# A GpSimd copy on 15 rows in place of two zero stores: backward pass of a decode block

## The chip, the cores and the metric

The kernel runs on one core of a Trainium2 chip. The core has five engines, TensorE (PE), VectorE (DVE), ScalarE (ACT), GpSimd (POOL) and SyncE (SP), and 16 DMA engines that move data between its on-chip memory and HBM. The metric is the time of one execution on the device in microseconds, taken as the median of the runs; smaller is better. Everything is bf16 unless said otherwise.

## The reference, cut to what matters

The forward pass is a residual block for one new token of each of 4 batches: layer norm, attention of 32 query heads over a cache of 8 kv-heads, and a gated MLP beside it. The attention looks at the last `W` = 1024 of `Sk` = 4096 cached keys alone.

```python
W = min(4096, max(256, Sk // 4))                       # 1024
k = jnp.repeat(k_cache[:, :, Sk - W:, :], rep, axis=1)
v = jnp.repeat(v_cache[:, :, Sk - W:, :], rep, axis=1)
p = _softmax(jnp.einsum("bhqd,bhkd->bhqk", q, k) * (Dh ** -0.5), axis=-1)
o = jnp.einsum("bhqk,bhkd->bhqd", p, v)
return x + A(layernorm(x)) + B(layernorm(x))
# ... (projections, gelu, transposes left out)

_out, _vjp = jax.vjp(_f, A_x, A_k_cache, A_v_cache, A_wq, A_wo, B_w_gate, B_w_up, B_w_down)
_grads = _vjp(grad_out)
return (_out0, *grads)
```

What must be written is the output and the gradient of every input. The gradients of the two caches, `out_2` (dk) and `out_3` (dv), have the caches' shape (4, 8, 4096, 128), 33.5 MB each. For the first `K0` = 3072 keys of every head the gradient is zero, because the attention never looks at them. These zero regions, 786,432 bytes for each batch and kv-head of each tensor, have to be written all the same.

## The kernel before: the parts that matter here

A zeroed tile in on-chip memory is the source of all zeros. One store writes the zero regions of two kv-heads of one batch: 128 partitions of 6144 elements (12,288 bytes) each. There are 32 such stores, listed in `zlist`, dk and dv in turn, batch by batch. They are issued by SyncE in small numbers between the other stores, to keep the DMA queue filled.

```python
ZR = 2
ZW = K0 * Dh * ZR // P                                  # 6144
ztile = const.tile([P, ZW], BF16, name="ztile")
zlist = deque((og, b, g) for b in range(B) for g in range(0, G, ZR) for og in (out_2, out_3))

def zero(n=1):
    for _ in range(min(n, len(zlist))):
        og, b, g = zlist.popleft()
        store(nc.sync, og[b, g:g + ZR, 0:K0, :].rearrange("g (m j) d -> m g (j d)", m=P // ZR), ztile[:], "zeros")

nc.gpsimd.memset(ztile[:], 0.0)
zero(3)
# ...
```

The helper `store` issues a DMA from the given engine; stores of the kind "zeros" and of the kind "rest" are declared to write disjoint parts.

```python
def store(eng, out, in_, kind):
    eng.nop()
    d = eng.dma_start(out=out, in_=in_)
    for k in ("rest", "zeros") if kind == "rest" else ("rest",):
        tc.declare_no_dep(d.ins, group=k, reason="stores write disjoint parts of the outputs")
    tc.add_to_no_dep_group(kind, d.ins)
    return d
```

The attention goes through the kv-heads in `NT` = 4 steps of two heads. A step transposes the keys and values, computes the softmax and its gradient, and leaves pieces of the large outputs in `bg`, from which `tick` takes some at later points. Pieces of dv and dk (`stg_dv`, `stg_dk`, 1 MB a store, three staging buffers) end with one zero store; those of the weight gradients are `osb_o` and `osb_q` (512 KB a store).

```python
def piece(g, j, held):                                  # of dv and dk
    # ... matmul into PSUM, evac into stg
    if j == JQ - 1:
        store(nc.sync, og[:, t * GP + g, K0:Sk, :].rearrange("b (m j) d -> m b (j d)", j=JB),
              stg[:].rearrange("p j d -> p (j d)"), "rest")
        zero()
# ...
for t in range(NT):
    kv_steps(t, 0, 0)
    # ...
    softmax(t)
    kv_steps(t, 1, 1)
    if t == NT - 1:
        zero(4)
    link(len(chain))
    softmax_d(t)
    link()
    odq(t, 0)                                           # ends with two multiplies on GpSimd (o_s)
    load_kv(t + 2, 1)                                   # nothing for the last two steps
    # ...
    fin(t)
    # ...
    (k0, k1), (o0, o1, q0, q1) = dvdk(t, 1), dw(t)
    for p in (k0, o0, k1, o1, q0, q1):
        bg.extend(p)
tick(len(bg))
zero(len(zlist))
# ... the sums for out_0 and out_1, stored from ScalarE with four rows each
```

GpSimd issues DMAs of its own in one place: the loads of the weights of steps 1 to 3 (`wo_sb`, `wq_sb`, 128 rows each).

Of the kernel before, what the change touches and what calls it, by code (L numbers as in the profile page):

```python
# [14 lines left out]
P = 128  # L15
# [3 lines left out]
def kernel(  # L19
# [28 lines left out]
    nc = tc.nc  # L48

    B, Sq, D = A_x.shape  # L50
    _, G, Sk, Dh = A_k_cache.shape
# [4 lines left out]
    K0 = Sk - W  # L56
# [4 lines left out]
    NT = G // GP  # L61
# [38 lines left out]
# [8 lines that stand above are left out]
# [12 lines left out]
    def load_w(t, eng=nc.gpsimd):  # L120
        pool = w_pool[t % 2]
        wo_t[t] = pool.tile([P, HG, D], BF16, name="wo_sb", tag="wo")
        eng.dma_start(out=wo_t[t][:], in_=wo_v[t])
        wq_t[t] = pool.tile([P, ND, CW], BF16, name="wq_sb", tag="wq")
        eng.dma_start(out=wq_t[t][:], in_=wq_v[t])

    def load_kv(t, k):
        if t >= NT:
            return
        d_, src, nm = ((k_t, A_k_cache, "kb"), (v_t, A_v_cache, "vb"))[k]  # L130
        for g in range(GP):
            tl = kv_pool[t % 2].tile([P, JB, Dh], BF16, name=nm, tag=nm)
            nc.sync.dma_start(out=tl[:].rearrange("p j d -> p (j d)"),
                              in_=src[:, t * GP + g, K0:Sk, :].rearrange("b (m j) d -> m b (j d)", j=JB))
            d_[(t, g)] = tl
# [20 lines left out]
    ZR = 2  # L156
    ZW = K0 * Dh * ZR // P
# [4 lines that stand above are left out]
        for _ in range(min(n, len(zlist))):  # L162
            og, b, g = zlist.popleft()
            store(nc.sync, og[b, g:g + ZR, 0:K0, :].rearrange("g (m j) d -> m g (j d)", m=P // ZR), ztile[:], "zeros")


    nc.gpsimd.memset(ztile[:], 0.0)
    zero(3)
    ident_f = const.tile([P, P], FP32, name="ident_f")
    nc.vector.tensor_copy(out=ident_f[:], in_=ident[:])  # L170
# [91 lines left out]
    def tick(n):  # L262
        for _ in range(min(n, len(bg))):
            bg.popleft()()
# [3 lines left out]
    def link(n=1):  # L268
        for _ in range(min(n, len(chain))):
            chain.popleft()()  # L270
# [173 lines left out]
    def odq(t, k):  # L444
        pT, blks = st[t][("PT", "dST")[k]], (v_t, k_t)[k]
        cols = pT[:].rearrange("p j (y s) -> p j s y", s=SL)
        for j in range(JB):
            q, jj = j // JQ, j % JQ
            for g in range(GP):
                nc.tensor.matmul(od_ps[g * 32:g * 32 + B * rep, k, g, :], lhsT=cols[:, jj, g * NQ + q, :],  # L450
                                 rhs=blks[(t, g)][:, j, :], start=(j == 0), stop=(j == JB - 1),
                                 tile_position=(0, g * 32))
        rows = attw.tile([P, GP, Dh], BF16, name="od_r", tag=f"od_r{k}", bufs=2)
        if k == 0:
            nc.vector.tensor_copy(out=rows[:], in_=od_ps[:, k])  # L455
        else:
            nc.scalar.activation(out=rows[:], in_=od_ps[:, k], func=ACT.Copy, scale=scale)
        st[t][("o", "dq")[k]] = rows
        if k == 0:

            o_s = attw.tile([P, GP, rep, Dh], BF16, name="o_s", tag="o_s", bufs=2)
            for g in range(GP):
                nc.gpsimd.tensor_tensor(out=o_s[:, g], in0=rows[:, g].unsqueeze(1).broadcast_to([P, rep, Dh]),  # L463
                                        in1=msk_r[:].unsqueeze(2).broadcast_to([P, rep, Dh]), op=ALU.mult)
            st[t]["os"] = o_s

    def odT(t, k):
        rows = st[t][("o", "dq")[k]]
        T_ps = transposes([rows[:, g, :] for g in range(GP)], "odT")
        rT = attw.tile([P, GP, B, rep], BF16, name="od_T", tag=f"od_T{k}")  # L470
        for g in range(GP):
            nc.vector.tensor_copy(out=rT[:, g].rearrange("p b r -> p (b r)"), in_=T_ps[:, g, g * 32:g * 32 + B * rep])
        st[t][("oT", "dqT")[k]] = rT
# [206 lines left out]
    for f4 in range(NF4):  # L680
        held = {}
        n = min(4, NF - 4 * f4)
# [34 lines left out]
    with tc.tile_pool(name="kv_b", bufs=GP, reuse_waits="tile") as kv_b, \  # L717
            tc.tile_pool(name="w_b", bufs=1, reuse_waits="tile") as w_b, \
            tc.tile_pool(name="stage", bufs=3, reuse_waits="tile") as stage:
        kv_pool[1], w_pool[1] = kv_b, w_b  # L720
        zero()
        pre(0)
        load_w(1)
        load_kv(1, 0)
        for t in range(NT):
            kv_steps(t, 0, 0)
            if t == 0:
                zero()
                load_kv(1, 1)
                zero()  # L730
            softmax(t)
            kv_steps(t, 1, 1)
            if t == NT - 1:
                zero(4)
            link(len(chain))
            softmax_d(t)
            link()
            odq(t, 0)
            load_kv(t + 2, 1)
            if t + 1 < NT:  # L740
                pre(t + 1)
            link(len(chain))
            odT(t, 0)
            odq(t, 1)
            load_kv(t + 2, 0)
            tick(2)
            odT(t, 1)
            fin(t)
            if t + 2 < NT:
                load_w(t + 2)  # L750
            (k0, k1), (o0, o1, q0, q1) = dvdk(t, 1), dw(t)
            for p in (k0, o0, k1, o1, q0, q1):
                bg.extend(p)
        tick(len(bg))
        zero(len(zlist))

        fin_ps = []
        for o in range(2):
            f_ps = ps_w.tile([B, ND, P], FP32, name="f_ps", tag="w")
            for c in range(ND):  # L760
                nc.tensor.transpose(f_ps[:, c, :], acc[:, o, c, :], ident_f[:])
            fin_ps.append(f_ps)
        acc_o = fin_ps[0][:].rearrange("b c p -> b (c p)")
        acc_d = attw.tile([B, P, ND], FP32, name="acc_d", tag="P_s")
        nc.vector.tensor_copy(out=acc_d[:].rearrange("b p c -> b c p"), in_=fin_ps[1][:])
        acc_d = acc_d[:].rearrange("b p c -> b (p c)")
        out_b = attw.tile([B, D], BF16, name="out_b", tag="pT")
        nc.vector.tensor_tensor(out=out_b[:], in0=acc_o, in1=x4[:], op=ALU.add)
        nc.scalar.dma_start(out=out_0.rearrange("b s d -> (b s) d"), in_=out_b[:])

        s1 = attw.tile([B, 1], FP32, name="s1", tag="m")
        nc.vector.reduce_sum(out=s1[:], in_=acc_d, axis=AX.X)
        pr = attw.tile([B, D], FP32, name="pr", tag="dS_s")
        s2 = attw.tile([B, 1], FP32, name="s2", tag="es")
        nc.vector.tensor_tensor_reduce(out=pr[:], in0=acc_d, in1=xn_f[:], scale=1.0, scalar=0.0,
                                       op0=ALU.mult, op1=ALU.add, accum_out=s2[:])
        nm1 = attw.tile([B, 1], FP32, name="nm1", tag="rr")
        nc.vector.tensor_scalar(out=nm1[:], in0=s1[:], scalar1=-1.0 / D, scalar2=None, op0=ALU.mult)
        nm2 = attw.tile([B, 1], FP32, name="nm2", tag="gs")
        nc.vector.tensor_scalar(out=nm2[:], in0=s2[:], scalar1=-1.0 / D, scalar2=None, op0=ALU.mult)  # L780
        nc.vector.scalar_tensor_tensor(out=pr[:], in0=xn_f[:], scalar=nm2[:, 0:1], in1=acc_d,
                                       op0=ALU.mult, op1=ALU.add)
        nc.vector.tensor_scalar(out=pr[:], in0=pr[:], scalar1=nm1[:, 0:1], scalar2=rstd[:, 0:1],
                                op0=ALU.add, op1=ALU.mult)
        dx_b = attw.tile([B, D], BF16, name="dx_b", tag="E_f")
        nc.vector.tensor_tensor(out=dx_b[:], in0=pr[:], in1=dy4[:], op=ALU.add)
        nc.scalar.dma_start(out=out_1.rearrange("b s d -> (b s) d"), in_=dx_b[:])
# [30 lines left out]
```

## Time and profile before

| | before |
|---|---|
| median of 3 runs | 283.08 us (283.03 to 283.26) |
| span of the profiled execution | 281.0 us |
| TensorE busy | 203.1 us (72%) |
| VectorE busy | 164.1 us (58%) |
| ScalarE busy | 117.8 us (42%) |
| GpSimd busy | 40.1 us (14%) |
| bytes moved by DMA | 112.12 MB, 399 GB/s over the span |
| HBM read, written | 30.68 MB, 81.01 MB |
| zero stores | 32, 1536 KB each, 18.1 us from issue to landing (median) |

The busy times are sums over the span; an engine that is busy for most of the span need not set the end. In the page's row "DMA" each digit is the mean busy share of the 16 DMA engines in one of 40 slices, so one engine that works alone hardly shows there; windows of the trace resolve it. In the list of queues, q1 carries the DMAs that SyncE issues, q10 those of ScalarE, q0 ("software") those of GpSimd, and q8 and q14 fetch instructions.

### The profile page before, as it was taken

The page shows a single profiled execution, that of the slowest core. Times are in us where ns is not written, and L with a number is a line of the kernel's source. Part 1 is how long each engine was busy: PE and PEld are TensorE (multiplying, and loading weights), DVE is VectorE, ACT ScalarE, POOL GpSimd, SP SyncE. Part 2 cuts the span into 40 slices and gives each one's busy share as a digit, 9 for nine tenths or more (in the row PEclk, how much of TensorE's full clock was granted, in tenths as well). Part 3 has the DMA queues.
Part 4 walks back from the last instruction along what each step waited for, and adds up shares of the span by engine and source line. Part 5 has one row for each costly group of instructions (what it writes and reads, how often), then busy time and mean ns, then how long its engine had stood idle before and what let it go on. Part 6 is the DMA issues. An engine that isn't in the chain of part 4 may idle for free.

```text
span 281.0 us, 6867 instructions
## 1 busy us (share of the span) xinstructions
PE 203.1 (72%) x2972; PEld 138.8 (49%) x2972; DVE 164.1 (58%) x313; ACT 117.8 (42%) x219; POOL 40.1 (14%) x40
## 2 busy tenths in 40 slices
PE   0276699959789889998999299898999599390000
PEld 0265476735456665566775156677556484140000
DVE  7946646645776655577666067767677728386000
ACT  2030386635035418764448056443866038370000
POOL 8600000007002150002250000223000400000000
PEclk9999589986999999999999969999999979977555
DMA  7999999999999999999999999999999999999990
GB/s 264 393 375 431 431 426 417 425 419 424 369 395 424 422 420 420 426 415 422 419 417 411 412 424 423 431 383 398 385 368 415 387 432 410 425 429 422 398 422 30
DMA packets 19565, 112.12 MB, mean 399 GB/s; under 512 B 1664, under 2 KB 4496, under 8 KB 11088
## 3 DMA queue, kind: packets, MB, share of 16 engines
q1 hardware_dynamic: 17744, 103.56, 89.6%
q0 software_dynamic: 1632, 6.29, 5.6%
q10 hardware_dynamic: 160, 1.84, 1.9%
q8 instruction: 23, 0.38, 0.5%
q14 instruction: 6, 0.05, 0.0%
HBM read 30.68 MB, written 81.01 MB: 397 GB/s over the span
## 4 chain that ended last, share of the span: by engine, by line
PE 47%; DMA 22%; DVE 16%; ACT 4%; issue 2%; SPq 0%; DVEq 0%; ACTq 0%
DMA out_dram<-stg_dv 13%; PE T_ps L279 8%; PE kv_ps L484 7%; DMA wd_sb<-in_B_w_down_dram 6%; PE S_ps L345 5%; PE od_ps L450 5%; DMA out_dram<-osb_g 4%; DVE T_sb L98 3%; DVE dS_s L367 2%; PE wdT_ps L279 2%; PE dwq_ps L520 2%; PE acc_ps L256 2%; PE dwd_ps L660 2%; DVE P_s L367 2%; PE wgT_ps L279 2%
## 5 line engine op out<-in xcount | busy, mean ns | idle before, releaser
L98 DVE COPY T_sb<-T_ps 128x1024 bf16<-128x1024 bf16 x64 | 44.1, 688 | 26.7 <-PE T_ps L279 26.5
L97 ACT CAST stg_dk<-kv_ps 128x512 bf16<-128x512 f32 x52 | 29.2, 588 | 31.2 <-PE kv_ps L484 12.4
L97 ACT CAST stg_dv<-kv_ps 128x512 bf16<-128x512 f32 x51 | 28.1, 588 | 24.9 <-PE kv_ps L484 24.3
L484 PE MATMUL kv_ps<-qmr,dS_s 128*128 128x512 bf16 x64 | 23.9, 414 | 11.3 <-ACT stg_dk L97 10.6
L463 POOL TENSOR_TENSOR o_s<-od_r,msk_r 128x512 bf16<-128x512 bf16 x8 | 9.1, 1157 | 110.2 <-DVE od_r L455 80.9
L484 PE MATMUL kv_ps<-domr,P_s 128*128 128x512 bf16 x64 | 21.3, 382 | 0.0
L279 PE MATMUL T_ps<-ident,vb 128*128 128x128 bf16 x256 | 20.3, 225 | 0.4 <-DVE T_sb L98 0.4
L279 PE MATMUL T_ps<-ident,kb 128*128 128x128 bf16 x256 | 20.4, 225 | 0.0
L279 PEld LDWEIGHTS <-kb 128*128 128x128 bf16 x256 | 17.5, 101 | 4.5 <-issue 1.3
L279 PEld LDWEIGHTS <-vb 128*128 128x128 bf16 x256 | 17.2, 101 | 5.0 <-issue 3.2
L97 ACT CAST osb_q<-dwq_ps 128x512 bf16<-128x512 f32 x25 | 14.6, 587 | 8.3 <-PE dwq_ps L520 7.4
L329 POOL TENSOR_TENSOR domr<-r,msk 128x1024 bf16<-128x1024 bf16 x4 | 7.6, 1892 | 71.2 <-DVE r L326 65.1
L97 ACT CAST osb_g<-dwg_ps 128x512 bf16<-128x512 f32 (+1 forms) x25 | 12.3, 544 | 12.3 <-PE dwg_ps L673 6.3
L97 ACT CAST osb_o<-dwo_ps 128x512 bf16<-128x512 f32 x24 | 13.9, 586 | 4.5 <-PE dwo_ps L505 2.9
L98 DVE CAST stg_dk<-kv_ps 128x512 bf16<-128x512 f32 x12 | 8.0, 688 | 12.0 <-DMA out_dram<-stg_dv 11.2
L98 DVE COPY wgT<-wgT_ps 128x1024 bf16<-128x1024 bf16 x14 | 9.6, 686 | 6.8 <-PE wgT_ps L279 6.8
L345 PE MATMUL S_ps<-T_sb,qm 128*32 128x256 bf16 x128 | 12.7, 387 | 0.6 <-DVE T_sb L98 0.5
L345 PE MATMUL S_ps<-T_sb,dom 128*32 128x256 bf16 x128 | 12.7, 388 | 0.1
L505 PE MATMUL dwo_ps<-dyr,o_s 128*128 128x512 bf16 x32 | 12.4, 413 | 0.3 <-ACT stg_dk L97 0.2
L98 DVE COPY woT<-woT_ps 128x1024 bf16<-128x1024 bf16 x16 | 11.0, 686 | 2.7 <-PE woT_ps L279 2.3
L484 PEld LDWEIGHTS <-dS_s 128*128 128x128 bf16 x64 | 6.2, 101 | 12.2 <-issue 11.1
L520 PE MATMUL dwq_ps<-od_r,xnm 128*128 128x256 bf16 x64 | 11.6, 274 | 0.3 <-ACT osb_q L97 0.2
(188 smaller groups left out, 385.0 us busy)
## 6 DMA issues: line engine op xcount, KB each, us to landing
out_dram<-ztile SPq DMA_DIRECT2D x32, 1536.0 KB, 18.1
kb<-in_A_k_cache_dram SPq DMA_DIRECT2D x8, 1024.0 KB, 17.4
vb<-in_A_v_cache_dram SPq DMA_DIRECT2D x8, 1024.0 KB, 20.7
out_dram<-stg_dv SPq DMA_DIRECT2D x8, 1024.0 KB, 13.0
out_dram<-stg_dk SPq DMA_DIRECT2D x8, 1024.0 KB, 20.8
out_dram<-osb_o SPq DMA_DIRECT2D x8, 512.0 KB, 17.4
out_dram<-osb_q SPq DMA_DIRECT2D x8, 512.0 KB, 13.8
out_dram<-osb_g SPq DMA_DIRECT2D x8, 448.0 KB, 14.3
```

What stands on the lines that cost most here:

```text
L97: return nc.scalar.copy(out=out, in_=in_)
L98: return nc.vector.tensor_copy(out=out, in_=in_)
L256: nc.tensor.matmul(ps[:, c, :], lhsT=lf(c), rhs=rhs, start=(k == 0), stop=(k == len(terms) - 1))
L279: nc.tensor.transpose(ps[:, i, :], a, ident[:])
L329: nc.gpsimd.tensor_tensor(out=mr[:].rearrange("p g q d -> p (g q) d"), in0=r4[:, k, :].unsqueeze(1).broadcast_to([P, SL, Dh]), in1=msk[:]. ...
L345: nc.tensor.matmul(ps[b * RB:(b + 1) * RB, :], lhsT=zt[:, b * GP + g, c0:c0 + RB], rhs=T_sb[:].rearrange("p (x b) -> p b x", b=B)[:, b, :] ...
L367: nc.vector.scalar_tensor_tensor(out=out[:], in0=src[:].unsqueeze(2).broadcast_to([P, WQ, B]), scalar=rr[:, 0:1], in1=mskb[:].unsqueeze(1) ...
L450: nc.tensor.matmul(od_ps[g * 32:g * 32 + B * rep, k, g, :], lhsT=cols[:, jj, g * NQ + q, :], rhs=blks[(t, g)][:, j, :], start=(j == 0), st ...
L463: nc.gpsimd.tensor_tensor(out=o_s[:, g], in0=rows[:, g].unsqueeze(1).broadcast_to([P, rep, Dh]), in1=msk_r[:].unsqueeze(2).broadcast_to([P ...
L484: nc.tensor.matmul(mps[:].rearrange("p q d -> p (q d)"), lhsT=src[:, j * P:(j + 1) * P], rhs=mr[:, g].rearrange("p q d -> p (q d)"), start ...
L505: nc.tensor.matmul(mps[:], lhsT=o_s[:, g].rearrange("p r d -> p (r d)")[:, i:rep * Dh:rep], rhs=dyr[:], start=True, stop=True)
L520: nc.tensor.matmul(mps[:, i].rearrange("p g d -> p (g d)"), lhsT=xnm[:, i2 * 2 + i, c * P:(c + 1) * P], rhs=dq_r[:].rearrange("p g d -> p ...
```

## The change

The last two zero stores of dv, kv-heads 4 to 7 of batch 3, are taken out of the list and written in another way. Of the first three of these heads, 15/16 of the zero region is copied from HBM to HBM: the source is the zero region of three heads of dk, written early in the kernel. That store is issued by GpSimd and has 15 rows outermost. Ahead of it GpSimd issues a store of 5 short rows and after it one of 12, from the zeroed tile; they fill part of the remaining sixteenth. The fourth head and what is left of the sixteenths are stored by SyncE at the very end. Near the end of the loop three zero stores are queued where four were. The work of the DMA engines is thereby divided unevenly on purpose: a transfer of 15 rows does not fall evenly on 16 engines.

```diff
+    def zero_15():
+        last = [z for z in zlist if z[0] is out_3][-2:]
+        for z in last:
+            zlist.remove(z)
+        b, g = last[0][1:]
+        assert last[1][1:] == (b, g + ZR)
+        dst = out_3[b, g:g + 2 * ZR]
+        KR = K0 // 16
+        k0 = 15 * KR
+
+        def rest(eng, n, h, k0, w):
+            store(eng, dst[h, k0:k0 + n * w, :].rearrange("(m j) d -> m (j d)", m=n), ztile[0:n if n == P else 8 * n - 7:1 if n == P else 8, 0:w * Dh],
+                  "zeros")
+
+        rest(nc.gpsimd, 5, 0, k0, 16)
+        s_, d_ = (x[0:3, 0:k0, :].rearrange("g (m j) d -> m g (j d)", m=15) for x in (out_2[0], dst))
+        store(nc.gpsimd, d_, s_, "zeros")
+        rest(nc.gpsimd, 12, 1, k0, 16)
+        return [lambda: rest(nc.sync, P, 3, 0, K0 // P), lambda: rest(nc.sync, 16, 0, k0 + 80, 7),
+                lambda: rest(nc.sync, 16, 2, k0, 12)]
...
             if t == NT - 1:
-                zero(4)
+                zero(3)
             link(len(chain))
             softmax_d(t)
             link()
             odq(t, 0)
+            if t == NT - 1:
+                rest = zero_15()
             load_kv(t + 2, 1)
...
         tick(len(bg))
         zero(len(zlist))
+        for z in rest:
+            z()
```

## The prediction

> **What bounds the kernel now.** I read the page first: the busy shares in 40 slices, then the DMA queues.
>
> ```profile
> PE   0276699959789889998999299898999599390000
> DMA  7999999999999999999999999999999999999990
> DMA packets 19565, 112.12 MB, mean 399 GB/s; under 512 B 1664, under 2 KB 4496, under 8 KB 11088
> ...
> q1 hardware_dynamic: 17744, 103.56, 89.6%
> q0 software_dynamic: 1632, 6.29, 5.6%
> ...
> q8 instruction: 23, 0.38, 0.5%
> ```
>
> The DMA row stands at 9 from the second slice to the last but one, while TensorE has nothing in the last four slices. The kernel is bound by what its 16 DMA engines move: 112.12 MB / 16 = 7.0 MB each. The chain of waits says the same: its last compute piece begins at 257.21 us, and its longest late piece is a wait for a store (233.63 us, lasting 11.70), after which a staging buffer comes free.
>
> So the end belongs to DMA. I next asked for engine busy time and DMA share in short windows there; the last two columns are DMA share and GB/s.
>
> ```profile
> 268.00:272.00 4.00, 0.00 (x0) 0.00 (x0) 0.00 (x0) 0.00 (x0) 0.00 (x0) 0.50 1.03 435
> ...
> 273.50:274.00 0.50, 0.00 (x0) 0.00 (x0) 0.00 (x0) 0.00 (x0) 0.00 (x0) 0.50 0.92 393
> 274.00:274.50 0.50, 0.00 (x0) 0.00 (x0) 0.00 (x0) 0.00 (x0) 0.00 (x0) 0.50 0.24 98
> 274.50:275.00 0.50, 0.00 (x0) 0.00 (x0) 0.00 (x0) 0.00 (x0) 0.00 (x0) 0.50 0.23 98
> 275.00:276.00 1.00, 0.00 (x0) 0.00 (x0) 0.00 (x0) 0.00 (x0) 0.00 (x0) 0.50 0.06 25
> ...
> 278.50:279.00 0.50, 0.00 (x0) 0.00 (x0) 0.00 (x0) 0.00 (x0) 0.00 (x0) 0.50 0.06 25
> 279.00:279.20 0.20, 0.00 (x0) 0.00 (x0) 0.00 (x0) 0.00 (x0) 0.00 (x0) 0.50 0.14 61
> 279.20:279.50 0.30, 0.00 (x0) 0.00 (x0) 0.00 (x0) 0.00 (x0) 0.00 (x0) 0.50 0.00 0
> ```
>
> This is the finding that everything below rests on. A share of 0.06 is 1/16: from 275 to 279.2 us **one DMA engine works alone**, at 25 GB/s. Thirteen engines are done at 273.7 to 274.2, two stragglers near 274.7, the last one at 279.2. The span ends at 281.03, so 1.8 us follow the last byte. What the lone engine still moves is shown by the DMA view of 276 to 279 us:
>
> ```profile
> DMA packets 6, 0.07 MB, mean 25 GB/s; under 512 B 0, under 2 KB 0, under 8 KB 0
> ```
>
> Those are packets of 12,288 B, the rows of the zero stores (128 rows of 12,288 B, 8 per engine). In the packet records each takes 460 ns and starts 457 ns after the one before. Counted back from the end, the lone engine starts its last 12 such packets when the main group is finishing: 12 x 12,288 = 147,456 B, or 5.5 us.
>
> **What the Trainium skill says.** (1) "DMA: Bandwidth & Descriptors", section "Why a DMA increments its semaphore by 16 and not by 1": a store issued from GpSimd whose outermost dimension allows only k < 16 engines runs on k consecutive engines from a round-robin cursor; all 16 if it allows 16. The section also names an exception in which a software-issued copy gets all 16, with the rows rounded up per engine. The trace before has only 128-row GpSimd transfers (six loads of weights), so it shows neither. (2) "Runtime: NRT & Kernel Launch", section "Instruction fetch mechanics": instructions arrive by DMA in blocks of 16 KiB. The trace agrees: 23 packets, 0.38 MB on q8, i.e. 16 KB each. If all fall on one engine they are 0.38 MB / 26.9 GB/s = 14 us of extra work there, which would explain a late engine; that they do is my guess. (3) The DMA page again, section "Latency and other measured facts": copies between HBM tensors reached 214 GB/s at best in one test. No transfer of this trace goes from HBM to HBM; its stores and loads run at 420 to 435 GB/s. This is the largest doubt here.
>
> **The change, part by part.** Removed: two of the 32 zero stores (the last four kv-heads of batch 3 in dv). Each engine sheds 2 x 8 x 12,288 = 196,608 B.
>
> Added, per engine:
> - the fourth head, one 128-row store of 6,144 B rows: 8 x 6,144 = 49,152 B on all 16;
> - two 16-row stores of 1,792 and 3,072 B rows: 4,864 B on all 16;
> - the copy: 3 heads x 15 rows of 192 x 128 x 2 = 49,152 B, one row of each head per engine: 147,456 B on 15 engines, nothing on one;
> - the 5 and 12 short rows of 4,096 B. With the cursor at c, the five take c to c+4, the fifteen take c+5 to c+19 and so **skip engine c+4**, the twelve take c+4 to c+15. The skipped engine gets 8,192 B, each other one 4,096 B. 5+15+12 = 32 puts the cursor back, so every execution repeats this.
>
> The skipped engine: 49,152 + 4,864 + 8,192 - 196,608 = -134,400 B, at 26.9 GB/s (12,288 B / 457 ns) -5.0 us. Each other: 49,152 + 4,864 + 147,456 + 4,096 - 196,608 = +8,960 B, +0.33 us.
>
> I choose to believe that the skipped engine is the late one: the 147,456 B that it is spared equal its 12 packets exactly, and 15 + 12 + 5 makes sense only as aiming. Then it ends at 279.2 - 5.0 = 274.2, the main group at 274.2 + 0.3 = 274.5, the stragglers at 274.7 + 0.4 = 275.1. The latest sets the end: 275.1 against 279.2 is -4.1 us. I give back 0.4 us for six transfers in place of two and the smaller packets: -3.7 us, **279.4 us**.
>
> What lies beside other work: the GpSimd issues come after its last two multiplies (221.24 us, 3.02 long), when GpSimd is idle for good. The copy then shares the engines with the zero stores queued at 219.74 (three instead of four), so no engine runs dry, and stg_dv waits behind +5.5 - 3.65 = +1.85 us of extra queue on the main engines but less on the late one, whose completion decides the 11.70 us wait. Compute should not end later than now, and it has 20 us of slack to the end anyway. The source zeros were written in the first tens of microseconds, so the new read-after-write wait costs nothing.
>
> **Rivals.**
> - *The copy runs at half speed*, because bytes read from and written to HBM count twice (skill, place 3). It then costs 147,456 B / 13.4 GB/s = 11.0 us instead of 5.5 on fifteen engines. They end at 274.5 + 5.5 = 280.0, the stragglers at 280.6: +1.4 us, about 284.5; if neighbouring stores hide part of it, 282 to 284. For it: HBM takes 81.0 MB of writes and 30.7 MB of reads already, 397 GB/s over the span. Against it: the packets of 12,288 B take 460 ns alone and 460 to 470 beside fifteen others, so what limits now is the engine and not HBM, and late stores have no loads beside them. I give it 0.30.
> - *The wrong engine is skipped*, or the exception applies (engine 15 is left out). The late engine then carries +0.33 us like the rest: about 283.4; with the half speed, 289. For it: nothing in the trace names the late engine's number. It is not one of the four that carry the four-row out_1 store, since its packet record runs through that time without a 1,024 B packet; the engine after them would fit a cursor starting at 0. I give it 0.12.
> - *The end is set by the queue and not the engines*: three short stores at the tail hold up SyncE. The waits of SyncE's queue are for slots of stores issued before; the tail still has two osb_q stores and a zero store (65,536 and 98,304 B per engine, 6.1 us) ahead of them. I think it costs under 0.3 us.
>
> **Range and chances.** The intended course (0.58) gives 278.6 to 279.9. A half-speed copy gives 282 to 285, a wrong engine 283.4 or more. That makes the low end 278.3, the high end 284.8, leaving out the wrong engine with a slow copy. A gain over 2% needs 277.4 us or less; perfect balance would be reached at about 5.5 x 15/16 = 5.2 us earlier, 277.9, so that is nearly excluded: 0.04. Within 2%: 0.90. Over 2% slower (288.7 or more): 0.06.
>
> **What the next profile would show.** Right: the stretch at a DMA share of 0.06 is gone and the share falls from 0.9 to zero within about 1 us, near 275; q0 has some 2.2 MB more; HBM reads rise by 2.2 MB to 32.9 and writes stay at 81.0; packets of the copy at about 27 GB/s. Half speed: the same sharp end but at 279 to 281, with long copy packets or a dip of GB/s after 224 us. Wrong engine: two lonely stretches, with one engine done about 5 us before the main group and one 5 us after it. The prediction fails altogether if the copy makes the staging wait so much longer that the queue runs dry before the last osb_q stores.

## The result and the profile after

| | before | changed | ratio (95% interval) |
|---|---|---|---|
| median, same chip | 283.05 us | 284.17 us | 1.0038 [1.002, 1.0055] |
| span of the profiled execution | 281.0 us | 282.4 us | |
| HBM read, written | 30.68, 81.01 MB | 32.89, 81.01 MB | |

The change costs 1.1 us; 3.7 us of gain were predicted. The number lies inside the range, but the course of things was another one. First the lines of the changed kernel's page that answer to those shown of before: span, DMA share in 40 slices, all packets, GpSimd's queue, HBM.

```profile
span 282.4 us, 6862 instructions
...
DMA  7999999999999999999999999999899998999990
...
DMA packets 19613, 112.12 MB, mean 397 GB/s; under 512 B 1746, under 2 KB 4594, under 8 KB 11347
...
q0 software_dynamic: 1760, 8.57, 7.7%
...
HBM read 32.89 MB, written 81.01 MB: 403 GB/s over the span
```

The bytes are as predicted: q0 has 2.28 MB more, HBM reads rise by 2.2 MB, the writes stay. The rate is not: two slices of the DMA row fall to 8. The next view is the table of windows at the end of the changed kernel; the last two columns are again DMA share and GB/s.

```profile
273.00:274.00 1.00, 0.00 (x0) 0.00 (x0) 0.00 (x0) 0.00 (x0) 0.00 (x0) 0.50 0.92 386
274.00:275.00 1.00, 0.00 (x0) 0.00 (x0) 0.00 (x0) 0.00 (x0) 0.00 (x0) 0.50 0.92 387
275.00:276.00 1.00, 0.00 (x0) 0.00 (x0) 0.00 (x0) 0.00 (x0) 0.00 (x0) 0.50 0.67 269
276.00:277.00 1.00, 0.00 (x0) 0.00 (x0) 0.00 (x0) 0.00 (x0) 0.00 (x0) 0.50 0.13 54
277.00:278.00 1.00, 0.00 (x0) 0.00 (x0) 0.00 (x0) 0.00 (x0) 0.00 (x0) 0.50 0.09 40
278.00:279.00 1.00, 0.00 (x0) 0.00 (x0) 0.00 (x0) 0.00 (x0) 0.00 (x0) 0.50 0.04 18
279.00:280.00 1.00, 0.00 (x0) 0.00 (x0) 0.00 (x0) 0.00 (x0) 0.00 (x0) 0.50 0.07 31
280.00:281.00 1.00, 0.00 (x0) 0.00 (x0) 0.00 (x0) 0.00 (x0) 0.00 (x0) 0.50 0.01 5
```

The stretch at about 1/16 is still there: one engine works alone from 277.2 to 280.4 us. The trace's records of single packets show more. They give a packet's queue, start, duration and size, but not its engine; packets are put on one engine by time, since the next one starts 3 to 4 ns before the one ahead ends. Read so, one engine is done at 273.3, fourteen between 275.4 and 277.2, the last at 280.44. (All ends of engines are given on the clock of the windows, as the end of the last packet. A window counts a packet where it starts.) A share of 0.92 at 273 to 275 is 15/16 with one engine already idle. **The copy spared an engine, but not the late one.**

The windows around the copy tell where the lower rate lies. GpSimd issues its three transfers at 224.4 to 226.2 us. Before:

```profile
228.00:232.00 4.00, 4.00 (x67) 2.80 (x64) 2.09 (x6) 2.57 (x6) 0.00 (x0) 0.93 1.04 428
232.00:236.00 4.00, 3.92 (x54) 2.30 (x52) 3.07 (x7) 3.02 (x7) 0.00 (x0) 1.00 1.00 421
236.00:240.00 4.00, 3.57 (x14) 1.27 (x13) 3.75 (x6) 3.86 (x8) 0.00 (x0) 1.00 1.02 420
```

And changed:

```profile
228.00:232.00 4.00, 3.77 (x61) 2.62 (x59) 1.85 (x6) 2.33 (x5) 0.00 (x0) 0.87 1.11 369
232.00:236.00 4.00, 3.91 (x57) 2.49 (x56) 3.07 (x6) 3.02 (x7) 0.00 (x0) 1.00 0.88 353
236.00:240.00 4.00, 3.57 (x13) 1.22 (x13) 3.81 (x7) 3.86 (x8) 0.00 (x0) 1.00 0.89 374
```

For 12 us the engines move 353 to 374 GB/s where they moved 420 to 428. Two things are seen in it. Copy packets of 49,152 B take 2,044 ns in the mean; the fastest take 1,815 ns, 27.1 GB/s, the same rate as a store. And from 231 to 235 us 14 of the 16 engines are at work in the mean, in the kernel before all 16; why some stand idle there is open. A copy at half speed is not seen. The 214 GB/s for copies between HBM tensors in the Trainium skill, "DMA: Bandwidth & Descriptors", section "Latency and other measured facts", which I had weighed as my largest doubt, were no limit here: the copy's 2.21 MB took 8.9 us beside the stores, 250 GB/s.

### The profile page after: what moved, and what is told of

Its sections match the earlier page's. It is cut to its first block, busy times and chain, and to the rows that moved or that the text cites. A ratio compares the mean times of both kernels' runs of the same rounds, so it can differ in the third digit from the quotient of the medians.

```text
span 282.4 us, 6862 instructions
## 1 busy us (share of the span) xinstructions
PE 202.5 (72%) x2962; PEld 138.7 (49%) x2972; DVE 164.4 (58%) x313; ACT 117.7 (42%) x219; POOL 41.9 (15%) x43
## 3 DMA queue, kind: packets, MB, share of 16 engines
HBM read 32.89 MB, written 81.01 MB: 403 GB/s over the span
## 4 chain that ended last, share of the span: by engine, by line
PE 43%; DMA 26%; DVE 16%; ACT 4%; issue 2%; SPq 0%; DVEq 0%; ACTq 0%
DMA out_dram<-stg_dv 13%; PE T_ps L302 8%; PE kv_ps L507 6%; DMA wd_sb<-in_B_w_down_dram 6%; PE S_ps L368 5%; PE od_ps L473 5%; DMA out_dram<-osb_g 4%; DMA out_dram<-osb_d 3%; DVE T_sb L98 3%; PE dwq_ps L543 2%; DVE dS_s L390 2%; PE acc_ps L279 2%; DVE P_s L390 2%; PE dwo_ps L528 2%; PE pT_ps L302 2%
## 5 line engine op out<-in xcount | busy, mean ns | idle before, releaser
L98 DVE COPY T_sb<-T_ps 128x1024 bf16<-128x1024 bf16 x64 | 44.1, 689 | 26.9 <-PE T_ps L302 26.7
L507 PE MATMUL kv_ps<-qmr,dS_s 128*128 128x512 bf16 x62 | 23.3, 412 | 13.3 <-ACT stg_dk L97 12.6
L507 PE MATMUL kv_ps<-domr,P_s 128*128 128x512 bf16 x58 | 19.7, 382 | 0.1
```

The costliest lines, as they stand in the source:

```text
L98: return nc.vector.tensor_copy(out=out, in_=in_)
L507: nc.tensor.matmul(mps[:].rearrange("p q d -> p (q d)"), lhsT=src[:, j * P:(j + 1) * P], rhs=mr[:, g].rearrange("p q d -> p (q d)"), start ...
```

## The experiments

Every ratio is to the kernel before on the same chip, with its 95% interval. Diffs are against the changed kernel unless said otherwise, cut to the lines that matter. In each, the zero regions are still written in full. "Index" counts the DMA engines from the one on which a transfer with few rows starts. If n short rows move the start by n, the 15 rows behind them leave out index n - 1.

### 1. Eight short rows ahead in place of five

```diff
-        rest(nc.gpsimd, 5, 0, k0, 16)
+        rest(nc.gpsimd, 8, 0, k0, 16)
...
-        rest(nc.gpsimd, 12, 1, k0, 16)
+        rest(nc.gpsimd, 9, 1, k0, 16)
```

> The short stores around the copy have 8 and 9 rows in place of 5 and 12, so that 8 + 15 + 9 is again 32. If a cursor decides which engine the copy leaves out, the left-out engine moves three places on (from c+4 to c+7): another engine then finishes early, and if that is the late one the time falls to about 279.5 us; if it is a third one the time stays near 284. If the rows of such stores always go to engines 0 to n-1, the left-out engine is the sixteenth in both kernels, nothing moves and the time is that of the changed kernel within 0.3 us, 283.9 to 284.4, with the same picture at the end: one engine early, one alone at the end.

Measured: 284.56 us, 1.0039 [1.0007, 1.007]; one engine alone until 280.3 us. Nothing is gained at this place either.

### 2. The copy on 16 rows

All three heads are copied whole, no short stores: no engine is spared.

```diff
-        rest(nc.gpsimd, 5, 0, k0, 16)
-        s_, d_ = (x[0:3, 0:k0, :].rearrange("g (m j) d -> m g (j d)", m=15) for x in (out_2[0], dst))
+        s_, d_ = (x[0:3, 0:K0, :].rearrange("g (m j) d -> m g (j d)", m=16) for x in (out_2[0], dst))
         store(nc.gpsimd, d_, s_, "zeros")
-        rest(nc.gpsimd, 12, 1, k0, 16)
```

> The whole zero regions of the three heads are copied from HBM by one GpSimd store of 16 rows, with no short stores: the same bytes on every engine as in the kernel before, so nothing is aimed at any engine. If a copy inside HBM costs what a store costs, the time is that of the kernel before with the last engine alone for some 5 us: 282.8 to 283.6. If the copy runs at half speed, every engine pays 5.5 us more and the time is 287.5 to 289.

Measured: 284.02 us, 1.0021 [1.0011, 1.0031], +0.6 us, late engine done at 280.37, where it was done at 279.58 in the kernel before. Copying costs 0.6 us in all, far from the 5.5 us of a half-speed copy. The rival "half speed" is out, and the remaining question is which engine is spared.

### 3. A probe: which rows fall on the late engine

In place of the change, GpSimd issues fifteen stores of 1 to 15 rows from on-chip memory and then fifteen copies of 1 to 15 rows within HBM; SyncE stores the rest of these heads at the end, with one store of 8 rows (against the kernel before).

```diff
+        for n in range(1, 16):
+            store(nc.gpsimd, dst[3, k0:k0 + 4 * n, :].rearrange("(m j) d -> m (j d)", m=n), z2[0:8 * n - 7:8, :], "zeros")
+            k0 += 4 * n
+        k0 = 0
+        for n in range(1, 16):
+            d_, s_ = (x[:, k0:k0 + 4 * n, :].rearrange("g (m j) d -> m g (j d)", m=n) for x in (dst[1:3], out_2[0][0:2]))
+            store(nc.gpsimd, d_, s_, "zeros")
+            k0 += 4 * n
```

> A probe of which engine is which. The last four heads of dv are written by 15 GpSimd stores of 1 to 15 rows of 1,024 B from on-chip memory, then 15 of 1 to 15 rows copied inside HBM (two heads, 1,024 B each), then SyncE stores of 128 rows, two of 16 rows and one of 8 rows. If rows go to engines 0 to n-1, the engine with index i shows in the trace i stores in which it has no row, then 15 - i in which it has one. If a cursor decides, each engine has rows in a wrapped pattern (store n takes the n engines after those of store n-1). The engine that ends last can then be named. I expect it to be none of the first four; the time is about that of the kernel before, 283 to 285 us.

Measured: one run, 284.65 us; late engine done at 280.80. It has a row of SyncE's 8-row store. In the packet records its rows in the two series differ in kind. An engine without a row in a copy of the second series shows a packet of 8 B in its place (105 in all, which is 14 + 13 + ... + 1), so that series can be read without gaps:

```
from on-chip memory   one unbroken run of the larger stores, about n = 5 to 15
from HBM, n = 2..15   - - - R - - R - R R R - R R      (R: a row on this engine)
```

The HBM series fits the second rule of the expectation and not the first: each copy takes n consecutive engines from where the one before ended. The on-chip series fits the first: every store begins at the same engine, so this engine has a row once n is large enough. This is the first sign that **a store of a few rows from on-chip memory does not move the place where the next copy starts**. One packet of 1,024 B is missing from the trace, so I didn't rest on that series alone. The place at which the HBM series begins (the copy of 2 rows at index 8 if the late engine is index 4) is not explained by this.

### 4. and 5. The copy on 7 rows and on 8 rows, nothing ahead

```diff
-        rest(nc.gpsimd, 5, 0, k0, 16)
-        s_, d_ = (x[0:3, 0:k0, :].rearrange("g (m j) d -> m g (j d)", m=15) for x in (out_2[0], dst))
+        k0 = 1120                                        # 8 rows: k0 = 1280, m=8
+        s_, d_ = (x[0:3, 0:k0, :].rearrange("g (m j) d -> m g (j d)", m=7) for x in (out_2[0], dst))
         store(nc.gpsimd, d_, s_, "zeros")
-        rest(nc.gpsimd, 12, 1, k0, 16)
```

> The copy has 7 rows of 3 x 40,960 B and no short stores; the rest of the three heads goes out in 128-row and 16-row stores. If rows go to engines 0 to n-1 and the late engine has index 7, engines 0 to 6 carry 122,880 - 53,760 = +69,120 B (+2.6 us) and engines 7 to 15 carry 53,760 B less (-2.0 us): the late one ends near 277.5 to 278, the low ones near 277.5, and the time falls by 1.3 to 2.0 us, to 281.1 to 281.8 where the kernel before has 283.1. If a cursor spreads the rows, different engines are spared in every execution and the times of one kernel scatter by several us. If the late engine is one of the first seven, it ends 2.6 us later: 285.7.

> The same with 8 rows. If the late engine has index 7 it is now among the eight that get a row: 122,880 - 61,440 = +61,440 B, +2.3 us, 285.5 to 286.0, slower than the kernel before where 7 rows are faster. If its index is 8 or more it is spared 2.3 us and both this kernel and the one with 7 rows are faster, 280.8 to 281.5. One step from 7 to 8 rows thus names the engine.

Measured with 7 rows: 286.89 us, 1.0114 [1.0086, 1.0142], all four runs between 286.5 and 287.3. The windows of its end:

```profile
277.00:278.00 1.00, 0.00 (x0) 0.00 (x0) 0.00 (x0) 0.00 (x0) 0.00 (x0) 0.50 0.12 51
...
279.00:280.00 1.00, 0.00 (x0) 0.00 (x0) 0.00 (x0) 0.00 (x0) 0.00 (x0) 0.50 0.06 23
280.00:281.00 1.00, 0.00 (x0) 0.00 (x0) 0.00 (x0) 0.00 (x0) 0.00 (x0) 0.50 0.07 27
281.00:282.00 1.00, 0.00 (x0) 0.00 (x0) 0.00 (x0) 0.00 (x0) 0.00 (x0) 0.50 0.07 27
```

The lone stretch runs to 282.16 us, 2.6 us later than in the kernel before (279.58): the late engine carries one of the seven rows and is **one of the first seven**. The gain that I thought possible for index 7 did not come. With 8 rows: 285.77 us, 1.0076 [1.0047, 1.0106], late end 281.76, which agrees. As the runs of each kernel agree among themselves, the start does not wander from one execution to the next.

### 6. The three heads stored by GpSimd from on-chip memory, 128 rows

```diff
-        rest(nc.gpsimd, 5, 0, k0, 16)
-        # ... (the copy and the 12 short rows)
+        store(nc.gpsimd, dst[0:2, 0:K0, :].rearrange("g (m j) d -> m g (j d)", m=P // 2), ztile[:], "zeros")
+        rest(nc.gpsimd, P, 2, 0, K0 // P)
```

> The three heads are written by GpSimd from the zeroed tile with 128 rows, at the place of the copy: the same queue and order as the copy on 16 rows, the same bytes per engine, but no reads from HBM. The copy on 16 rows measured 1.0021 of the kernel before, +0.6 us. If reading from HBM costs these 0.6 us, this kernel is level with the kernel before (ratio 0.999 to 1.001). If the second queue or the moved order costs them, it shows the same 1.002.

Measured: 283.71 us, 1.0017 [1.0004, 1.003], +0.5 us, late end 279.87. Without any read from HBM the cost is nearly that of experiment 2 (+0.6). So most of this half microsecond seems to come from the other order and the second queue, not from the copying; the interval, which begins at 1.0004, doesn't exclude a share of the reads.

### 7. to 10. Four, three, six and seven short rows ahead

```diff
-        rest(nc.gpsimd, 5, 0, k0, 16)
+        rest(nc.gpsimd, 4, 0, k0, 8)                     # then 3, 6, 7
...
-        rest(nc.gpsimd, 12, 1, k0, 16)
+        rest(nc.gpsimd, 13, 1, k0, 8)                    # then 14, 11, 10
```

> The copy is aimed one engine lower than in the changed kernel: 4 short rows before it and 13 after. In the probe the late engine has no row in the HBM stores of 9 and 13 rows and has one in those of 8, 10, 11, 12, 14 and 15. Stores that follow each other round the 16 engines fit this only if that engine is the twelfth after the start of the HBM part, and 119 rows before it make it the fourth (c+3). The store of 7 rows and that of 8 both slowed it, which agrees. So a copy that leaves out c+3 should spare it: -5.0 us on the late engine, +0.3 us on the rest, about 0.6 us for the second queue: the share of 0.06 at the end disappears and the time is 279.3 to 280.3 us, a ratio of 0.987 to 0.991. If rows go to engines 0 to n-1 whatever stands before, the time is that of the changed kernel, 284.

> 3 short rows before the copy and 14 after, so c+2 is left out. If the late engine is c+3 it keeps its copy and the time stays at 284 to 284.5, with one engine alone at the end. If my count of the probe is off by one in this direction, the gain is here: 279.3 to 280.3.

> 6 short rows before the copy and 11 after, so c+5 is left out. If the late engine is c+3 the time stays at 284 to 284.5. If the HBM copies count from another start, and four-row stores of ScalarE are on the first four engines so that the late one is the fifth to seventh, this kernel could gain: 279.3 to 280.3.

> 7 short rows before the copy, 10 after: c+6 is left out. Left-out engines c+2, c+3, c+4, c+5 and c+7 did not help, while stores on c to c+6 and on c to c+7 slowed the late engine by what a row costs; in the trace of the changed kernel the late engine has a row of the 12-row store, so it is in c+4 to c+15. Only c+6 is in all of these. The late engine then carries 5.0 us less and the main group sets the end: 279.3 to 280.3 us, ratio 0.987 to 0.991, and no stretch at a share of 0.06 over 1 us. If the late engine is not a fixed one but whichever falls behind, or if rows are not given in turn, nothing changes: 284 to 285.

| short rows ahead | time | ratio (95% interval) | row ahead on the late engine | copy rows on it |
|---|---|---|---|---|
| 3 | 284.89 us | 1.0048 [1.0032, 1.0063] | no | 3 |
| 4 | 284.58 us | 1.004 [1.0025, 1.0054] | no | 3 |
| 5 (the change) | 284.17 us | 1.0038 [1.002, 1.0055] | yes | 3 |
| 6 | 284.83 us | 1.0034 [1.0014, 1.0053] | yes | 3 |
| 7 | 284.58 us | 1.0039 [1.0019, 1.0059] | yes | 3 |

Experiments 7 and 10 expected a gain, 8 and 9 held one possible; none came. By experiment 4 (seven rows) the late engine is among the first seven, and it is not among the first four, if those are the four that carry the prediction's four-row store. If n short rows moved the start, n = 5, 6 or 7 would have to spare it. None does: all five versions give it its three copy rows. The count of packets says the same. An engine that the copy spares comes early to its row of the last store. With a start moved by n it has such a row, and n + 1 short packets would come early; the five traces show 3, 4, 5, 6 and 7 of them up to 231.6 us and no other before 237.6. Hence short rows from on-chip memory, 3 to 7 of them, don't move the start; the copy begins at the same index each time, and if that is index 0, it leaves out the last engine. The column of rows ahead then points to the late engine: a store from index 0 reaches it with 5 rows and not with 4, so it would be **the fifth, index 4**, just where 5 + 15 aims. This column is the weaker part: where the short rows pass, near 229 us, several engines fit by time. Experiments 12 and 13 test the place by itself.

### 11. All fifteen rows from on-chip memory

If copies and on-chip stores count differently, 15 rows read from 15 partitions of the zeroed tile might obey the short rows ahead.

```diff
+        rest(nc.gpsimd, 7, 0, k0, 8)
+        for h in range(3):
+            # ... from the second head on: 9 and 8 short rows ahead
+            store(nc.gpsimd, dst[h, 0:k0, :].rearrange("(m a j) d -> m a (j d)", m=15, a=4),
+                  ztile[0:113:8, :].unsqueeze(1).broadcast_to([15, 4, ZW]), "zeros")
+        rest(nc.gpsimd, 10, 1, k0, 8)
```

> The same engine is left out, but the 15 rows come from the zeroed tile (15 partitions, 12,288 B each, four times per row), one store per head, with stores of 9 and 8 short rows between them so that each leaves out the same engine. If the source of the copy doesn't matter, the time is that of the HBM copy with the same aim, within 0.4 us. If 15 partitions read by 15 engines are slow to read, the stores take longer than 1.8 us per 49,152 B and the time is 1 us or more above it.

Measured: 290.81 us, 1.025 [1.0185, 1.0316]. The windows after the issue show why:

```profile
225.00:235.00 10.00, 9.28 (x152) 7.02 (x153) 4.64 (x12) 4.66 (x9) 4.99 (x10) 0.83 1.01 353
235.00:245.00 10.00, 6.71 (x48) 2.65 (x46) 5.71 (x10) 5.44 (x10) 0.00 (x0) 1.00 1.00 272
245.00:255.00 10.00, 0.00 (x0) 0.00 (x0) 0.18 (x1) 0.20 (x1) 0.00 (x0) 0.59 1.00 374
```

The engines are busy all the time (share 1.00) yet move 272 GB/s. GpSimd's packets of 12,288 B take 763 ns in the mean against 460 elsewhere, those of SyncE beside them about 580. The slow packets hide the aim, so the run says nothing on it. Whether the small number of partitions or their spacing of eight slows them was not separated. It is a reason to take the source of 15 rows from HBM, as the change does.

### 12. and 13. The short rows copied within HBM too: five and four

The probe says that copies within HBM follow each other round the engines. So the short rows are copied as well, and the aim of 5 + 15 + 12 should hold.

```diff
-        rest(nc.gpsimd, 5, 0, k0, 16)
-        # ...
-        rest(nc.gpsimd, 12, 1, k0, 16)
+        def copy(n, h, k1, w):
+            s_, d_ = (x[0:h, k1:k1 + n * w, :].rearrange("g (m j) d -> m g (j d)", m=n) for x in (out_2[0], dst))
+            store(nc.gpsimd, d_, s_, "zeros")
+        copy(5, 2, k0, 8)                                # second version: 4
+        copy(15, 3, 0, KR)
+        copy(12, 2, k0 + 40, 8)                          # second version: 13, k0 + 32
```

> The short rows before and after the copy are copied inside HBM too (two heads, rows of 2 x 2,048 B), still 5, 15, 12. In the traces so far the late engine has a row of short stores from on-chip memory with 5, 6, 7 rows and none with 3 and 4: it is the fifth engine, and such stores start at the first engine, whatever came before; the copy of 15 rows then also started at the first and left out the last, in every version. In the probe the copies inside HBM, and they alone, follow each other round the engines. So 5 rows copied inside HBM should move the start of the 15 rows to the sixth engine and leave out the fifth, the late one: 279.3 to 280.3 us, ratio 0.986 to 0.991, no stretch at a share of 0.06 over 1.5 us at the end. If the start cannot be moved at all: 284 to 285.

> The same with 4, 15, 13: the fourth engine is left out. If the late one is the fifth, this stays at 284 to 284.8, with one engine alone at the end, beside a gain of the version with 5. If it gains and the version with 5 does not, the late one is the fourth.

**Five:** 280.69 us against 283.81, ratio 0.9894 [0.9866, 0.9922], better than both kernels. Its end, and the line of its chain of waits that carries the wait for a staging buffer:

```profile
273.00:274.00 1.00, 0.00 (x0) 0.00 (x0) 0.00 (x0) 0.00 (x0) 0.00 (x0) 0.50 0.91 387
274.00:275.00 1.00, 0.00 (x0) 0.00 (x0) 0.00 (x0) 0.00 (x0) 0.00 (x0) 0.50 1.04 436
275.00:276.00 1.00, 0.00 (x0) 0.00 (x0) 0.00 (x0) 0.00 (x0) 0.00 (x0) 0.50 0.87 359
276.00:277.00 1.00, 0.00 (x0) 0.00 (x0) 0.00 (x0) 0.00 (x0) 0.00 (x0) 0.50 0.22 85
277.00:278.00 1.00, 0.00 (x0) 0.00 (x0) 0.00 (x0) 0.00 (x0) 0.00 (x0) 0.50 0.01 3
278.00:279.00 1.00, 0.00 (x0) 0.00 (x0) 0.00 (x0) 0.00 (x0) 0.00 (x0) 0.50 0.00 0
```

```profile
233.80 11.11 DMA out_dram<-stg_dv
```

The lone stretch is gone. In its packet records six short packets come early (up to 232.3 us) and eleven late (from 238.9 on); in the changed kernel these are five and twelve. Six is what a moved start leaves: the five of the first copy, and on the spared engine, which has no long rows, the one of the last.

**Four:** 284.29 us, 1.0022 [1.0011, 1.0034]; here five short packets come early, four and one, so the start has moved too. Another engine, by the count the one next to it, is spared, and the late one is alone again:

```profile
276.00:277.00 1.00, 0.00 (x0) 0.00 (x0) 0.00 (x0) 0.00 (x0) 0.00 (x0) 0.50 0.12 48
277.00:278.00 1.00, 0.00 (x0) 0.00 (x0) 0.00 (x0) 0.00 (x0) 0.00 (x0) 0.50 0.06 25
278.00:279.00 1.00, 0.00 (x0) 0.00 (x0) 0.00 (x0) 0.00 (x0) 0.00 (x0) 0.50 0.06 25
279.00:280.00 1.00, 0.00 (x0) 0.00 (x0) 0.00 (x0) 0.00 (x0) 0.00 (x0) 0.50 0.07 31
280.00:281.00 1.00, 0.00 (x0) 0.00 (x0) 0.00 (x0) 0.00 (x0) 0.00 (x0) 0.50 0.03 13
```

One row more or less ahead makes 1.3% of the time, if those rows are copies. The short copies differ from the short stores in form as well (two heads to a row), so the runs don't show whether the source alone or the form makes the difference.

## Why the prediction was wrong

**Right.** The bound is DMA, and one late engine sets the end: sparing that one, and no other, moves the time (experiments 12 and 13). It is the engine after the first four, as the four-row store had hinted. The copy doesn't run at half speed, and the bytes moved came out as counted.

**The failing step** is "I choose to believe that the skipped engine is the late one". Behind it stood "with the cursor at c, the five take c to c+4, the fifteen take c+5 to c+19". I took that rule from the Trainium skill, "DMA: Bandwidth & Descriptors", section "Why a DMA increments its semaphore by 16 and not by 1", for all three transfers. It holds for the copies (probe, experiments 12 and 13). It doesn't hold for the short stores of 3 to 7 rows from on-chip memory: they leave the cursor where it was and, as far as the packets show, start at index 0, as that section's exception would have them. So the rival that I gave 0.12 was the case, in its second form: the last engine is left out, and the late one carries the copy like the rest. Five rows are the right number for a late engine of index 4: as copies they gave 0.9894, as stores 1.0038. As stores they had no effect on the start.

**The sizes.** For that rival I had 283.4 us. The late engine ended 0.9 us later (280.44 against 279.58) and the kernel took 1.1 us more. The prediction gave it 8,960 B, +0.33 us. It got more: stores of 5 and of 12 rows that both start at index 0 both have a row for index 4, so 13,056 B, +0.49 us at 26.9 GB/s. About 0.5 to 0.6 us is the other order and the second queue (+0.5 without any copy, +0.6 with a full one). Together that is the 1.1 us. The prediction's ends of engines (274.2, 274.7, 279.2) are about 0.4 us early: the last packet before starts at 279.11 and ends at 279.57. Its differences stay, but 1.5 us and not 1.8 follow the last byte.

**The rest of the intended course** can be read in the version with five copied rows. It gained 1.06%, 3.0 us of 283.05, where I had 3.7. Its main group ended at 275.7 to 276.5 and the last engine at 277.2, against 275.1 in the prediction, which is 275.5 on this clock. The 0.4 us given back for more transfers was too little. The 0.5 us of moved order belongs there; copy packets of 2,099 ns in that version in place of 1,815 would be 3 x 0.28 = 0.9 us for an engine with three of them. How these and the idle time at 231 to 235 us share the 1.7 us was not separated.

**The staging wait.** I expected it not to grow. In the changed kernel it did, as its chain of waits shows. The late engine has 57,344 B more to carry ahead of that store (three copy rows and two short ones for one zero store), 2.1 us at 26.9 GB/s:

```profile
233.86 13.93 DMA out_dram<-stg_dv
```

It was 11.70, and is 11.11 when the late engine is spared. It moved the last compute piece from 257.2 to 260.1 us, still 20 us before the last byte, so it cost nothing by itself. Yet the last two SyncE stores of osb_q were issued from 262.55 on in place of 259.52, and the spared engine stood idle for about 1.4 us between 263 and 267 us. It was done about 2 us before the others and not 5. A sign that I had named for a wrong engine thus came smaller than I had said; the idle time is only a part of the difference.

**My guess on the cause of the late engine** fell. As far back as its packets were followed, from 158 to 279 us, they hold no fetch of instructions. In the kernel before it is slower per packet for part of that time: 500 ns for 12,288 B against 462 on the others at 160 to 200 us, about 490 against 466 at 225 to 245, but 461 after 260. Why it is slower stays open; nothing was tried on it.

## What to carry to other kernels

When the end is set by DMA, look for the last microseconds with a share of 1/16: one engine can be late by several microseconds (4.4 here), and its place among the engines can be found by transfers of few rows. To give an engine less work through the number of rows, keep the source memory and the form of all transfers in the chain the same, and look in the packet records for the engine that was spared: the rule for the start was not the same for copies within HBM and stores from on-chip memory. That a plan is aimed at one engine is no sign that it hits it: keep a good part of the chances for a miss until a trace shows where the rows land.

## What the runs showed of the hardware

- Copies that GpSimd issues within HBM, with n rows, took n consecutive engines from where the last one ended. Its stores of 3 to 7 rows from on-chip memory didn't move that place, and their packets fit a start at the first engine each time. Five short rows: 0.9894 as copies, 1.0038 as stores.
- A store of 8 rows from on-chip memory may be different: in experiment 1, with 8 and 9 short rows, nine short packets come early, as if the start had moved by 8. That would spare index 7, which is not the late engine. With the unexplained start of the probe's HBM series this stays open.
- 49,152 B from HBM to HBM took one engine 1,815 ns at best, 27.1 GB/s, no slower than zeros from on-chip memory (12,288 B in 457 ns, 26.9 GB/s); in the mix with stores the mean was 2,044 ns.
- Fifteen engines reading 15 partitions, eight apart, took 763 ns for 12,288 B, against 460 from 128 partitions; the kernel lost 2.5%.
- The late engine was up to 8% slower per packet than the others at 160 to 200 us (500 against 462 ns) and no slower after 260 us (461 ns).
